# First loads, idle run and late steps of an FNet-plus-mixer kernel: another order of queues, places and turns

## The chip, the cores and the metric

The kernel runs on one core of a Trainium2 chip. The time is device microseconds of one execution, from the program's start to its end; a figure for a kernel is the median of several executions. Engines are called by their names: TensorE (PE, with its weight loads as PEld), VectorE (DVE), ScalarE (ACT), GpSimd (POOL) and SyncE (SP), which here only issues transfers. Transfers that SP and ScalarE issue go to a queue of their own each; those that GpSimd issues go to a third.

## What is computed

The input `x` is one matrix of 2048 tokens by 640 channels. With `xn` the layer norm of `x` over the channels, the output is the sum of three terms:

```python
xn = _layernorm(x)
# A: FNet. Real(DFT_seq(DFT_hid(layernorm-ed x))), as real matrices
a = einsum("bsd,ed->bse", xn, dft_hid_re);  b = einsum("bsd,ed->bse", xn, dft_hid_im)
A = einsum("ts,bse->bte", dft_seq_re, a) - einsum("ts,bse->bte", dft_seq_im, b)
# B: Mixer over the tokens, shared by the channels
h = _layernorm(xn)
u = gelu(einsum("bsd,sf->bdf", h, w1) + b1)          # F = 1728
B = transpose(einsum("bdf,fs->bds", u, w2) + b2)
return x + A + B
```

All is float32. There are four large products: two with the sequence matrices (2048 by 2048 each), one with the hidden matrices (640 by 640), and the two layers of the mixer (2048 by 1728).

## The kernel before

**Arithmetic.** Each float32 operand is cut in two: a high part, which ScalarE makes (`high`, line 151), and a low part, which VectorE makes by subtraction (`low`, line 154). A block product is three TensorE matmuls (`three`, lines 162, 163 and 165): high by high, high by low, low by high. Beyond the first columns, products of 2 by 2 blocks are done with seven instead of eight block products; the sums and differences of blocks that this needs are made on VectorE (`sub`, line 157). An operand block that comes from memory and is cut for one use is a *piece*.

**Steps.** The program is one list of steps. A step is one piece and the matmuls that use it. `turn_of(i)` (line 1215) writes out, for step `i`, in this order: transfers (`loads`), reads of finished banks (`reads`), sums (`sums`), the high cut of the piece for step `i + 2`, `extras`, `timed` actions, one or no waiting *job*, the low cut of that piece, and the matmuls of step `i`. So pieces are cut two steps ahead. Each engine executes its share in exactly this order. Jobs prepare operands for a later stage; they stand in one first-in-first-out list and are taken one for each turn, where the tables `JOBS_AT` and `LONG_AT` allow it. A `None` in the list uses up a turn and does nothing.

**Stages.** The first columns of the sequence product (lines 487 to 577, steps 0 to 9), six further groups of columns and the last halves (`columns`, line 579), the hidden product (`hidden`, stage "hid", written with `row_steps`), the first mixer layer in two passes (`up(0, r)` and `up(1, r)`, r from 0 to 6), and the second in two passes (`down(0, t)`, `down(1, t)`). The sequence product goes out to DRAM as `y`, in part by accumulating stores on GpSimd's queue, and is read again by the hidden stage (line 1033). Half results of the mixer's first layer are kept in DRAM as `up`.

**The start.** The word list `START` (line 49) writes out the first turns by hand. Among its words: `x0` loads row block 0 of `x` and `b0` the first piece of the sequence matrix (`load`, line 494); `M`, `A`, `R` take a row's statistics, their aggregate and the root; `D` and `H` write the row's high parts, `L` its low parts, `N` normalizes it; `T` and `B` cut a piece's high and low part; `P` runs matmuls, with `-0-1` or `-2` naming which of the three. Ahead of `START` stand a few instructions: the second half of row block 0 on ScalarE's queue (line 135), two clears on VectorE, a dummy activation that loads ScalarE's table (line 142), and `WARM` matmuls on a cleared tile, the idle run (line 148).

**Places.** Large tiles live in fixed places: `slab0` to `slab7`, which hold the normalized rows' parts first and the moving operands of the later stages after; `xa` and `xb` for pieces; `ca`, `cb`, `v` and the three parts `x0`, `x1`, `x2` of `xb` for pairs of row blocks. A new tile in a place waits until the old one's last reader is done. The long group of columns (the fourth) needs two more pairs of pieces than its place holds; they stand in a slab under the name `more` (line 598). The hidden matrices wait in a slab as `hids` (line 766) and are cut to operands by `matrices` (line 774). Lines 1165 to 1196 say which slab or place each of these takes, and when.

**Second passes.** `rows_again` (line 784) loads rows of `x` once more (line 790), normalizes them a second time and cuts them for the first mixer layer. In `up(1, r)` the result is added to what pass 0 left in DRAM by an accumulating load (line 1050), and `gelu` follows some turns later (lines 1052 to 1066). For r from 4 to 6 the result goes to DRAM again (line 1070), and `hidden_rows` (line 795) fetches it for the second pass of the last layer.

Of the kernel before, what the change touches and what calls it, by code (L numbers as in the profile page):

```python
# [8 lines left out]
F32 = mybir.dt.float32  # L9
R32 = mybir.dt.float32r  # L10
BF16 = mybir.dt.bfloat16
AF = mybir.ActivationFunctionType
ALU = mybir.AluOpType

P = 128
S = 2048
D = 640
# [8 lines left out]
CH = 512  # L26
NC = S // CH
H2 = D // 2
# [3 lines left out]
WARM = 10  # L32
# [17 lines left out]
    x0 b0 x1 b1 b2 x4 b3 x5 b4 x2 x3 b5 x6 x7 b6 b7  # L50
    M0 A0 R0 T0 D0 O0 V0 H0 B0 M1 A1 T1 B1 N0 R1 T2 L0 O1 V1 H1 B2 P0-0-1 P1-0-1 P0-2 P1-2
# [26 lines left out]
def fnet_plus_mixer(  # L78
# [56 lines left out]
    nc.scalar.dma_start(x_in[0][:, H2:], x_rows[0][:, H2:])  # L135
# [3 lines left out]

    nc.vector.memset(one, 1.0)  # L140
    nc.gpsimd.memset(eps, EPS)
    nc.scalar.activation(one, one, AF.Abs_reciprocal_sqrt)
    nc.gpsimd.tensor_scalar(idea, eps, EPS, eps, op0=ALU.add, op1=ALU.mult)
    idle = keep.tile([P, CH], BF16, name="idle", tag="slab7")
    nc.vector.memset(idle, 0.0)
    psum = [acc.tile([P, CH], F32, name=f"psum{i}") for i in range(8)]
    for i in range(WARM):
        nc.tensor.matmul(psum[7], idle[:, :P], idle, start=True, stop=True)
# [338 lines left out]
    def first_columns():  # L487
# [6 lines left out]
        def load(i):  # L494
            m, k = FIRST[i][:2]
            nc.sync.dma_start(raw[:, FIRST_AT[i], :], dft_seq[m * NC, k])
# [33 lines left out]
        def row(k):  # L530
            if k == 0:
                nc.sync.dma_start(x_in[0][:, :H2], x_rows[0][:, :H2])
            else:
                nc.sync.dma_start(x_in[k], x_rows[k])
# [27 lines left out]
        def whole_row(k):  # L562
# [13 lines left out]
            "L": lambda k: first_rows(k, 1),  # L576
        }

    def columns(g, h, c):
# [13 lines left out]
        def load(name, q):  # L593
            i, m = int(name[1]) - 1, int(name[2]) - 1
            k = 8 * h + q + 4 * i
            if q >= 4:
                if not more_pairs:
                    more_pairs.append(keep.tile([P, 2, 2, 2, CH], F32, name="more", tag="slab1"))
                k = APART + q - 4 + 4 * i
            nc.sync.dma_start(b(name, q), dft_seq[m * NC + c, k])  # L600
# [163 lines left out]
    def load_matrices(qs):  # L764
        if 0 in qs:
            t = keep.tile([P, 3, 2, D], F32, name="hids", tag="slab0")
            raw_hid.update({q: t[:, q] for q in range(3)})
        for q in qs:
            if q > 2:
                raw_hid[q] = place["v"]()  # L770
            for m in range(2):
                nc.sync.dma_start(raw_hid[q][:, m, :], dft_hid[m, q])
# [22 lines left out]
    def hidden_rows(q, at):  # L795
        return from_place(at, lambda v: nc.sync.dma_start(v, part_up[4 + q]), [], "down1", q, f"slab{q}")
# [240 lines left out]
    def up(stage, r, at):  # L1037
# [6 lines left out]
        def end(c):  # L1044
# [19 lines left out]
            late = 5 if tail else 2 if r >= 4 else 1  # L1064
            for i in range(2):
                timed[e + 6 + late + i].append(lambda i=i: gelu(i))
            if r < 4:
                timed[e + 9].append(lambda: jobs.extend(moving_of("down0", r, f"slab{4 + r}", lambda: c)))
            else:
                timed[e + 8 + late].append(lambda: nc.gpsimd.dma_start(part_up[r], c))  # L1070
# [4 lines left out]
        def by_dram(i):  # L1075
            def run(row, half, b):

                at = i in (5, 7)
                t = place["x1"]()[:, (r + (i in (5, 4))) % 2, at * H2 : (at + 1) * H2]
# [82 lines left out]
    for q in range(3):  # L1162
# [3 lines left out]
        [j for q in range(4) for j in matrices(q, f"slab{(q + 1) % 4}")] + factors_again() + [lambda: load_matrices((4,))]  # L1166
# [6 lines left out]
    for q in range(4):  # L1173
        get, changes, rest = rows_again(0, q, "v")
        timed[s_hid - 1].append(lambda js=[get, None, None] + changes + rest: jobs.extend(js))
# [13 lines left out]
    for r in range(NF2):  # L1189
        up(1, r, ("x2", "ca", "cb", "v", "x0")[r % 5])  # L1190
# [3 lines left out]
    gets_hid, _, rests_hid = zip(*(hidden_rows(q, ("x0", "v")[q % 2]) for q in range(3)))  # L1194
    for q in range(2):
        timed[s_down + 7 + 2 * q].append(lambda q=q: jobs.append(gets_hid[q]))
# [98 lines left out]
```

## Time and profile before

| | |
|---|---|
| Median of 3 executions | 867.07 us (866.6 to 867.45) |
| The profiled execution | 867.25 us, with a span of 865.5 us from the first to the last instruction |
| TensorE busy | 860.3 us, 4894 matmuls |
| VectorE busy | 693.4 us |
| ScalarE busy | 525.4 us |
| Transfers | 154.44 MB, mean 178 GB/s |

How to read the rows that follow. A row of the timeline has the start and the length in us, the engine, the line of the kernel, the operation, the tile written and the tile read, shapes, how many instructions are drawn together, and in brackets the idle time before it with what ended that idle time. "SPq", "ACTq" and "POOLq" are the issuing of transfers. A row of the waits names who waited, for whom, and the total, number and longest of these waits. A row of the windows names a stretch, its length, the busy time and number of instructions of PE, PEld, DVE, ACT and POOL, the granted clock, the share of the transfer engines and their GB/s. A row of the transfers by issue ends with the KB of one and the median time from issue to landing.

### The profile page before, as it was taken

The page shows a single profiled execution, that of the slowest core. Times are in us where ns is not written, and L with a number is a line of the kernel's source. Part 1 is how long each engine was busy: PE and PEld are TensorE (multiplying, and loading weights), DVE is VectorE, ACT ScalarE, POOL GpSimd, SP SyncE. Part 2 cuts the span into 40 slices and gives each one's busy share as a digit, 9 for nine tenths or more (in the row PEclk, how much of TensorE's full clock was granted, in tenths as well). Part 3 has the DMA queues.
Part 4 walks back from the last instruction along what each step waited for, and adds up shares of the span by engine and source line. Part 5 has one row for each costly group of instructions (what it writes and reads, how often), then busy time and mean ns, then how long its engine had stood idle before and what let it go on. Part 6 is the DMA issues. An engine that isn't in the chain of part 4 may idle for free.

```text
span 865.5 us, 13906 instructions
## 1 busy us (share of the span) xinstructions
PE 860.3 (99%) x4894; PEld 788.9 (91%) x4894; DVE 693.4 (80%) x1172; ACT 525.4 (61%) x975; POOL 162.6 (19%) x224
## 2 busy tenths in 40 slices
PE   9999999999999999999999999999999999999998
PEld 6888888888888888888999999999999999999998
DVE  7798868758768888677877788888678978987887
ACT  6765576763555555547565556676667866555654
POOL 4222131210020211122110101111312221101211
PEclk9999999999999999999999999999999999999999
DMA  9949596795382746879586766665687789766776
GB/s 345 360 100 270 185 252 228 161 285 160 98 186 29 201 98 140 206 115 190 111 182 155 165 138 196 189 170 162 143 187 169 162 233 241 183 142 125 157 170 149
DMA packets 90293, 154.44 MB, mean 178 GB/s; under 512 B 9008, under 2 KB 37424, under 8 KB 89968
## 3 DMA queue, kind: packets, MB, share of 16 engines
q0 software_dynamic: 25008, 57.52, 36.8%
q1 hardware_dynamic: 64928, 95.80, 33.9%
q8 instruction: 38, 0.62, 0.3%
q14 instruction: 31, 0.25, 0.1%
q10 hardware_dynamic: 288, 0.25, 0.1%
HBM read 99.96 MB, written 58.82 MB: 183 GB/s over the span
## 4 chain that ended last, share of the span: by engine, by line
PE 98%; DMA 1%; ACT 0%; DVE 0%; issue 0%; DVEq 0%; ACTq 0%
PE psum L163 32%; PE psum L162 32%; PE psum L165 31%; PE psum L508 3%; DMA y<-c 1%; DMA x<-in_x 0%; ACT piece L151 0%; DVE st L223 0%; ACT shid L151 0%; ACT c L671 0%; ACT pair L954 0%; DVE pair L946 0%; DVEq L1291 0%; DVE mv L226 0%; ACT near L232 0%
## 5 line engine op out<-in xcount | busy, mean ns | idle before, releaser
L151 ACT ACTIVATE piece<-pieces 128x512 fp32r<-128x512 f32 (+2 forms) x472 | 295.6, 626 | 222.1 <-PE psum L165 139.2
L154 DVE TENSOR_TENSOR piece<-pieces,piece 128x512 fp32r<-128x512 f32 (+4 forms) x496 | 327.2, 660 | 128.2 <-ACT piece L151 124.9
L162 PE MATMUL psum<-piece,n 128*128 128x512 f32 x540 | 210.1, 389 | 0.0
L163 PE MATMUL psum<-piece,n 128*128 128x512 f32 x540 | 210.1, 389 | 0.0
L165 PE MATMUL psum<-piece,n 128*128 128x512 f32 x540 | 210.1, 389 | 0.0
L162 PE MATMUL psum<-sup,piece 128*128 128x320 f32 x392 | 120.8, 309 | 0.0
L162 PE MATMUL psum<-sdown,piece 128*128 128x320 f32 x392 | 120.8, 309 | 0.0
L163 PE MATMUL psum<-sdown,piece 128*128 128x320 f32 x392 | 120.8, 309 | 0.0
L163 PE MATMUL psum<-sup,piece 128*128 128x320 f32 x392 | 120.8, 309 | 0.0
L163 PEld LDWEIGHTS psum<-piece,n 128*128 128x128 f32 x540 | 101.4, 188 | 21.1
L165 PEld LDWEIGHTS psum<-piece,n 128*128 128x128 f32 x540 | 101.3, 188 | 21.1
L162 PEld LDWEIGHTS psum<-piece,n 128*128 128x128 f32 x540 | 101.3, 188 | 20.9
L157 DVE TENSOR_TENSOR pieces<-pieces 128x512 f32<-128x512 f32 (+3 forms) x142 | 111.9, 793 | 3.0
L165 PE MATMUL psum<-sup,piece 128*128 128x320 f32 x368 | 113.7, 309 | 0.0
L165 PE MATMUL psum<-sdown,piece 128*128 128x320 f32 x368 | 113.7, 309 | 0.0
L485 POOL DMA_DIRECT2D y<-c x65 | 56.0, 891 | 255.2 <-DVE c L683 153.9
L162 PE MATMUL psum<-shid,piece 128*128 128x320 f32 x280 | 86.6, 309 | 0.4 <-ACT pair L954 0.4
L165 PE MATMUL psum<-shid,piece 128*128 128x320 f32 x280 | 86.5, 309 | 0.0
L163 PE MATMUL psum<-shid,piece 128*128 128x320 f32 x280 | 86.5, 309 | 0.0
L162 PEld LDWEIGHTS psum<-sup,piece 128*128 128x128 f32 x392 | 73.6, 188 | 0.0
L162 PEld LDWEIGHTS psum<-sdown,piece 128*128 128x128 f32 x392 | 73.6, 188 | 0.0
L163 PEld LDWEIGHTS psum<-sdown,piece 128*128 128x128 f32 x392 | 73.6, 188 | 0.0
(129 smaller groups left out, 1110.5 us busy)
## 6 DMA issues: line engine op xcount, KB each, us to landing
pieces<-in_dft_seq SPq DMA_DIRECT2D x120, 256.0 KB, 5.3
y<-c POOLq DMA_DIRECT2D x105, 256.0 KB, 4.8
pieces<-in_w SPq DMA_DIRECT2D x88, 256.0 KB, 4.0
out<-pair POOLq DMA_DIRECT2D x38, 320.0 KB, 5.9
pieces<-y SPq DMA_DIRECT2D x32, 320.0 KB, 4.5
pieces<-in_w SPq DMA_DIRECT2D x32, 192.0 KB, 2.7
out<-in_x SPq DMA_DIRECT2D x16, 320.0 KB, 8.0
up<-pair POOLq DMA_DIRECT2D x8, 640.0 KB, 3.2
```

The costliest lines, as they stand in the source:

```text
L151: nc.scalar.activation(hi, src, AF.Copy)
L154: nc.vector.tensor_sub(lo, src, hi.bitcast(F32))
L157: nc.vector.tensor_sub(to, a, b)
L162: nc.tensor.matmul(psum, wh, mh, start=first, stop=False, skip_group_check=True)
L163: nc.tensor.matmul(psum, wh, ml, start=False, stop=last and wl is None, skip_group_check=True)
L165: nc.tensor.matmul(psum, wl, mh, start=False, stop=last, skip_group_check=True)
L485: nc.gpsimd.dma_start(y_part[m][c][:, j, :], t, accum_op=ALU.add)
L508: nc.tensor.matmul(banks[m, j], channels(k, j)[rows], w[cols], start=n == 0 and k == begin, stop=n == 2 and k == end, skip_group_check=True,)
```

## The change

The diff touches the start and the order of some late steps. No matmul of the computation is added or taken away.

- **Row block 0.** Both halves are loaded on SP's queue, one after the other. The first piece goes on ScalarE's queue instead of SP's, behind a one-column clear of its place on VectorE, so its issue waits for that clear.
- **Start order.** The table-loading activation becomes a word of its own, `W0`, after `b0`. The second piece is loaded before row block 1, and its cuts `T1 B1` are written ahead of row 1's statistics `M1 A1`.
- **Idle run.** The cleared tile has 128 instead of 512 columns and is cleared first. The run has 14 matmuls instead of 10: ten of 512 columns, which read the tile four times over, and four of 128.
- **Slabs.** The late pairs' pieces (`more`) take slab 0 and the hidden matrices slab 1; the cut matrices' slabs go along.
- **Later turns.** The two gelus of `up(1, r)` are one step later except at the last r; so are the job list's next entries and the store. In `rows_again(0, q)` the load comes one job later, and the second normalization as late as before. The second fetch of `hidden_rows` is two steps later.
- **Places.** `x0`, `x1`, `x2` and `v` trade roles in `up` and `hidden_rows`.

```diff
-WARM = 10
+WARM = 14
...
-    x0 b0 x1 b1 b2 x4 b3 x5 b4 x2 x3 b5 x6 x7 b6 b7
-    M0 A0 R0 T0 D0 O0 V0 H0 B0 M1 A1 T1 B1 N0 R1 T2 L0 O1 V1 H1 B2 P0-0-1 P1-0-1 P0-2 P1-2
+    x0 b0 W0 b1 x1 b2 x4 b3 x5 b4 x2 x3 b5 x6 x7 b6 b7
+    M0 A0 R0 T0 D0 O0 V0 H0 B0 T1 B1 M1 A1 N0 R1 T2 L0 O1 V1 H1 B2 P0-0-1 P1-0-1 P0-2 P1-2
...
-    nc.scalar.dma_start(x_in[0][:, H2:], x_rows[0][:, H2:])
...
+    idle = keep.tile([P, P], BF16, name="idle", tag="slab7")
+    nc.vector.memset(idle, 0.0)
     nc.vector.memset(one, 1.0)
     nc.gpsimd.memset(eps, EPS)
-    nc.scalar.activation(one, one, AF.Abs_reciprocal_sqrt)
...
-    idle = keep.tile([P, CH], BF16, name="idle", tag="slab7")
-    nc.vector.memset(idle, 0.0)
...
     for i in range(WARM):
-        nc.tensor.matmul(psum[7], idle[:, :P], idle, start=True, stop=True)
+        n = 4 if i < WARM - 4 else 1
+        to = psum[7][:, : n * P].rearrange("p (n c) -> p n c", n=n)
+        nc.tensor.matmul(to, idle, idle.unsqueeze(1).to_broadcast([P, n, P]), start=True, stop=True)
...
-            nc.sync.dma_start(raw[:, FIRST_AT[i], :], dft_seq[m * NC, k])
+            to = raw[:, FIRST_AT[i], :]
+            if i == 0:
+                nc.vector.memset(to[:, :1], 0.0)
+            (nc.sync if i else nc.scalar).dma_start(to, dft_seq[m * NC, k])
...
-                nc.sync.dma_start(x_in[0][:, :H2], x_rows[0][:, :H2])
+                for i in range(2):
+                    nc.sync.dma_start(x_in[0][:, i * H2 : (i + 1) * H2], x_rows[0][:, i * H2 : (i + 1) * H2])
...
+            "W": lambda k: nc.scalar.activation(one, one, AF.Abs_reciprocal_sqrt),
...
-                    more_pairs.append(keep.tile([P, 2, 2, 2, CH], F32, name="more", tag="slab1"))
+                    more_pairs.append(keep.tile([P, 2, 2, 2, CH], F32, name="more", tag="slab0"))
...
-            t = keep.tile([P, 3, 2, D], F32, name="hids", tag="slab0")
+            t = keep.tile([P, 3, 2, D], F32, name="hids", tag="slab1")
...
-            late = 5 if tail else 2 if r >= 4 else 1
+            late = 5 if tail else 3 if r >= 4 else 2
...
-                timed[e + 9].append(lambda: jobs.extend(moving_of("down0", r, f"slab{4 + r}", lambda: c)))
+                timed[e + 10].append(lambda: jobs.extend(moving_of("down0", r, f"slab{4 + r}", lambda: c)))
...
-                t = place["x1"]()[:, (r + (i in (5, 4))) % 2, at * H2 : (at + 1) * H2]
+                t = place["x1" if stage else "x2"]()[:, (r + (i in (5, 4))) % 2, at * H2 : (at + 1) * H2]
...
-        [j for q in range(4) for j in matrices(q, f"slab{(q + 1) % 4}")] + factors_again() + [lambda: load_matrices((4,))]
+        [j for q in range(4) for j in matrices(q, f"slab{(0, 2, 3, 1)[q]}")] + factors_again() + [lambda: load_matrices((4,))]
...
-        timed[s_hid - 1].append(lambda js=[get, None, None] + changes + rest: jobs.extend(js))
+        timed[s_hid - 1].append(lambda js=[None, get, None] + changes + rest: jobs.extend(js))
...
-        up(1, r, ("x2", "ca", "cb", "v", "x0")[r % 5])
+        up(1, r, ("x0", "ca", "cb", "v", "x2")[r % 5])
...
-    gets_hid, _, rests_hid = zip(*(hidden_rows(q, ("x0", "v")[q % 2]) for q in range(3)))
+    gets_hid, _, rests_hid = zip(*(hidden_rows(q, ("v", "x0")[q % 2]) for q in range(3)))
...
-        timed[s_down + 7 + 2 * q].append(lambda q=q: jobs.append(gets_hid[q]))
+        timed[s_down + 7 + 4 * q].append(lambda q=q: jobs.append(gets_hid[q]))
```

## The prediction, made before the changed kernel ran

> **What bounds the kernel now.** I read the page's busy rows first, then the waits of TensorE, then the start and the one stall in the middle at full resolution, and last the chain of waits.
>
> ```profile
> span 865.5 us, 13906 instructions
> PE 860.3 (99%) x4894; PEld 788.9 (91%) x4894; DVE 693.4 (80%) x1172; ACT 525.4 (61%) x975; POOL 162.6 (19%) x224
> PE psum L148 <- DVE idle L145: 1.2, 1, 1.2
> PE psum L508 <- ACT piece L151: 0.4, 1, 0.4
> PE psum L162 <- ACT pair L954: 0.4, 1, 0.4
> 860.00:863.00 3.00, 2.32 (x16) 2.05 (x14) 2.37 (x7) 0.00 (x0) 0.00 (x0) 1.00 0.47 163
> 600.00:700.00 100.00, 100.00 (x684) 100.00 (x683) 81.33 (x138) 71.97 (x143) 24.75 (x30) 1.00 0.74 173
> ```
>
> TensorE is busy 860.3 of 865.5 us. It waits three times in all: 1.2 us before the idle run, 0.4 us between the idle run and the first product, 0.4 us once more at 404.9 us. The rest is the tail: the last matmul ends near 862.3 us (2.32 us of work in the stretch from 860), then the last output goes out. The window from 600 to 700 us, where most moved steps lie, has 100.00 of 100.00 us busy with 684 matmuls, 0.146 us each. No edit removes a real product, so the only time that can be won is in these gaps and in the 4.16 us of idle matmuls ahead of the first product. Much more can be lost: any new wait of TensorE counts in full.
>
> The start, in order of time (start, length, engine, what):
>
> ```profile
> 0.75 0.41 ACTq L135 DMA_DIRECT2D x<-in_x  x1
> 0.76 0.39 SPq L532 DMA_DIRECT2D x<-in_x  x1
> 0.91 0.27 DVE L145 MEMSET idle<- 128x256 uint32 x1
> 1.19 1.28 ACT L142 ACT_TABLE_LOAD   x1 [1.19 <-PEq L1284]
> 1.24 4.16 PE L148 MATMUL psum<-idle 128*128 128x512 bf16 x10 [1.24 <-DVE idle L145]
> 3.69 0.89 DVE L223 BATCH_NORM_STATS2 st<-x 128x6 f32<-128x320 f32 x2 [2.50 <-DMA x<-in_x]
> 4.61 0.21 DVE L226 BATCH_NORM_AGGREGATE mv<-st 128x2 f32<-128x12 f32 x1
> 4.91 0.29 ACT L232 ACTIVATE near<-mv,eps 128x1 f32<-128x1 f32 x1 [2.23 <-DVE mv L226]
> 5.12 0.61 ACT L151 ACTIVATE piece<-pieces 128x512 fp32r<-128x512 f32 x1
> 5.80 10.54 PE L508 MATMUL psum<-piece,n 128*128 128x512 f32 x45 [0.40 <-ACT piece L151]
> x<-in_x ACTq DMA_DIRECT2D x1, 160.0 KB, 3.1
> x<-in_x SPq DMA_DIRECT2D x1, 160.0 KB, 2.9
> 9.50:20.00 10.50, 10.50 (x47) 8.70 (x47) 8.64 (x25) 8.38 (x15) 5.94 (x15) 1.00 1.05 393
> ```
>
> The first product at 5.80 us hangs on a chain that begins with row 0: both halves are issued at once on two queues and land 2.9 and 3.1 us later, at about 3.7 and 3.8 us; then come two statistics, the aggregate, the root on ScalarE, and only behind the root in ScalarE's order the cut of the first piece. The idle run ends at 5.40 us, so row 0 sets the start, by 0.40 us.
>
> **The change, part by part.**
>
> *Row 0 in turn, first piece on ScalarE's queue.* The two halves shared the engines, so each took the time of both. One half is 160 KB, 0.41 us at the 393 GB/s of the row above. Alone in front, the first half should land up to 0.4 us earlier, and the first statistic start at about 3.3 us instead of 3.69. The second half is issued one SP issue (0.39 us) later, just when the first statistic (half of 0.89 us) is busy; it may land at 3.7 us and cost nothing. The aggregate, the root and the cut follow 0.4 us earlier at best: first product at 5.40 us. Against it: the first piece (256 KB) now sits in the other queue, issued behind a one-column memset on VectorE, at about 1.2 us, the moment of the second half's issue. If the engines alternate between the two, the second half lands where it did, at 3.8 us, and behind the 4.1 us at which the second statistic began, so nothing is won; if the piece goes ahead, 0.3 us is lost. I take 0.3 us won, because the second half follows the first in a queue that is already flowing while the other must start, and keep -0.3 and +0.4 as ends.
>
> The Trainium skill (DMA: Bandwidth & Descriptors, section Issuing engines are not separate DMA queues) says that transfers started by different engines run on the same 16 DMA engines and interleave; the two halves landing 0.2 us apart agrees. By that rule the piece takes turns with the second half, the gain would be near nothing, and the sum would be that of the first rival below.
>
> *Longer idle run.* The idle tile is cleared first and at a quarter of its size, so the run can begin at about 0.95 to 1.0 us instead of 1.24. Ten long matmuls are 4.16 us; the four short ones are a quarter of 0.42 us each, 0.42 us at most. The run then ends between 5.2 (1.0 plus 4.16, with four short ones hidden in the modelled end of the last long one) and 5.6 us. It could itself hold back the first product by up to 0.2 us against 5.40. With the chain at 5.50 and the run at about 5.5 us, 0.3 us stays.
>
> *Table load behind the piece's issue (W0), second piece ahead of row 1.* ScalarE now issues the piece (0.41 us) before the table load of 1.28 us and its 0.20 us dummy; they end near 3.1 us, and the next use is the root at 4.5 us. The cover is that 1.4 us; without it the root is late one for one. SP issues as many transfers as before: one half in, one piece out. Row 1 goes behind the second piece (256 KB, 0.65 us at 393 GB/s), and so do its statistics on VectorE behind that piece's low cut. This is the second gate of the start:
>
> ```profile
> 6.50 0.88 DVE L223 BATCH_NORM_STATS2 st<-x 128x6 f32<-128x320 f32 x2
> 7.73 0.69 DVE L154 TENSOR_TENSOR piece<-pieces,piece 128x512 fp32r<-128x512 f32 x1
> 8.71 0.90 DVE L154 TENSOR_TENSOR n<-x,n 128x512 fp32r<-128x512 f32 x2 [0.29 <-ACT x L278]
> 9.45 6.69 PEld L508 LDWEIGHTS psum<-piece,n 128*128 128x128 f32 x30 [0.19 <-DVE n L154]
> ```
>
> The low half of row 0 (8.71 us) already arrives with nothing to spare: the weight load at 9.45 us waited 0.19 us for it. It waits for ScalarE's normalization, which hangs on row 0 as well and moves with it; on VectorE it is queued behind the second piece's cut (0.69), row 1's statistics (0.88) and aggregate (0.21). If row 1 starts them at 7.05 to 7.3 us (6.50 plus 0.65, or a little later behind the cut), they end by 8.4 us and the low half still moves ahead by 0.3 us; if row 1 comes 0.5 us later still, the low half is back at 8.9 us and eats the gain and 0.2 us more. I take 0.05 us off. Start in all: 0.25 us won, between 0.3 lost and 0.4 won.
>
> *Row loads one job later.* The stall at 404.9 us:
>
> ```profile
> 397.18 7.56 DMA y<-c
> 404.84 0.44 ACT L954 ACTIVATE pair<-psum 128x320 f32<-128x320 f32 x1 [1.25 <-DMA y<-c]
> 400.96 2.62 SPq L790 DMA_DIRECT2D pair<-in_x  x2
> 403.63 8.60 SPq L1033 DMA_DIRECT2D pieces<-y  x4
> SPq L790 <- DVE shid L154: 7.9, 1, 7.9
> y<-c POOLq DMA_DIRECT2D x105, 256.0 KB, 4.8
> q8 instruction: 38, 0.62, 0.3%
> 400.00:404.90 4.90, 4.90 (x33) 4.59 (x31) 3.85 (x6) 2.51 (x5) 1.73 (x2) 1.00 1.01 181
> ```
>
> The first block of the new stage (line 954) writes where accumulating stores of y were read from, and one of those took 7.56 us where the median is 4.8. Meanwhile SP stood 7.9 us before the row load of line 790, which waits for VectorE to leave its place; the next read of y (line 1033) stood behind it until 403.63. Moved one job, the row load comes after that read in SP's order. The row load itself does not start later, since VectorE, not the order, releases it at 400.96; but the read of y (320 KB) is free to run before it, into the very time of the slow store, with the engines full (share 1.01). So the edit can lengthen what it sits beside. Ends: at the median the store lands at 402.0 us, ScalarE is free at 403.6, and the 0.40 us stall is gone; with 320 KB wholly in front at 181 GB/s the store is 1.8 us later. A second influence: 38 instruction loads (0.62 MB) serve, by their number, some 257 of the 9,788 TensorE instructions each; four more matmuls with their weight loads are 8 instructions, and move each such load ahead by 8/2 x 0.225 us = 0.9 us. One may be what held the store; which way it turns is open. I take no change, nearest to the row as it is, with -0.4 and +1.8 us as ends. Behind a late line 954 on ScalarE stands the cut of the piece two steps on, 0.7 us, with over a step (15 x 0.146 = 2.2 us) to spare. The normalizations that use the loaded rows come as late as before, two jobs behind instead of three; if a load is not there, ScalarE stands up to one step, 2.2 us, against the same reserve.
>
> *Late pieces in slab 0, matrices in slab 1.* SP stood for the old place:
>
> ```profile
> SPq L600 <- PE psum L165: 7.3, 1, 7.3
> 170.00:177.50 7.50, 7.50 (x35) 6.21 (x34) 3.43 (x5) 6.41 (x11) 2.60 (x3) 1.00 0.84 157
> 177.50:195.00 17.50, 17.50 (x78) 14.48 (x78) 10.41 (x21) 11.05 (x22) 2.50 (x4) 1.00 1.03 331
> L1055 ACT ACTIVATE pairs<-pairs,b_sb 128x640 f32<-128x640 f32 x6 | 4.9, 822 | 0.0
> SPq L796 <- DMA up<-pairs: 11.0, 1, 11.0
> ```
>
> Slab 0 is left one step earlier than slab 1, six matmuls of 0.225 us (17.50 over 78), so SP moves on 1.35 us earlier. TensorE did not wait there (17.50 of 17.50), so nothing is won; if the earlier burst pushed another load back by 1.35 us, the two-step lead of the cuts covers it.
>
> *Gelus and stores a step later, places swapped, later read of the hidden rows.* No instruction is added. A gelu of 0.82 us moves by one step of 12 x 0.146 = 1.75 us, and the jobs behind it by one turn; the store behind it on the POOL queue too. The hidden rows that SP waited 11.0 us for are asked for two steps later. Cover: their first use is seven or more steps away; uncovered, each would cost up to a step, 1.75 us. Taken at nothing.
>
> Sum: 867.25 us is the profiled execution's own time (span 865.5). 867.25 - 0.25 + 0 = 867.0. That execution lies 0.18 above the median of 867.07, so against the median: **866.8 us**.
>
> **Rivals.**
> 1. The start gains nothing (chance 0.2): the piece's turns with row 0's second half, or row 1 in front of the low half, give it back. For it: the shared landing times and the 0.19 us wait; against it: VectorE's 0.29 us idle before the low half. 867.07 + 0 to 0.2: 867.15 us.
> 2. Slower: the read of y now runs ahead of the row load into the slow store at 397 us (chance 0.25). It decides as soon as that store lands later than 405 us. For it: the 7.9 us SP wait that held it back; against: the earlier instruction load. Stall 1.2 to 2.2 instead of 0.4, less the start: 867.6 to 868.6, at half of it 868.0 us.
> 3. The stall vanishes, the store landing before 403.6 us (chance 0.15): 866.8 - 0.4 = 866.4 us.
> 4. The products begin slow (chance 0.05). Idle matmuls come every 0.41 us, products of the same width every 0.23 (3.70 over 16, the row below), and the turn comes during the idle run. Were it to come as much later again, 3.3 us into the products, 1.65 us is lost: 868.4 us. The same can strike before.
>
> ```profile
> 1.24:4.50 3.26, 3.26 (x8) 1.18 (x9) 0.81 (x2) 1.44 (x2) 0.00 (x0) 1.00 0.80 256
> 5.80:9.50 3.70, 3.70 (x16) 2.95 (x17) 3.27 (x8) 2.69 (x5) 2.17 (x5) 1.00 1.03 380
> ```
>
> The Trainium skill (TensorE: Matmul & The Clock Gate, section What's actually happening) has the gate decide in windows of some 3.4 us that run free of the kernel; that makes rival 4 a matter of the run's luck, and the shift of 0.24 us in the idle run's start next to irrelevant.
>
> **How the numbers follow.** The forecast has 0.35, the rivals 0.2, 0.25, 0.15 and 0.05. A difference under 0.2%, 1.7 us, is about what a measurement of this kernel can't tell from none. Faster by more would need more than the stalls at 404.9 and 5.4 us together, so 0.03. Slower by more (over 868.8) takes the upper part of rival 2, rival 4 at its worst, or a stall that none of my rows shows: 0.12. Range: from rival 3 with the best start (866.1) down a little for spread, to the top of rival 2: 866.0 to 868.7. The likeliest case alone: 866.5 to 867.2.
>
> **What would show it.** Right: first statistic near 3.3 us, first product at 5.4 to 5.6 us with no gap behind the idle run, the weight load of the low half near 9.2 us, the read of y ahead of the row load near 397 us, a stall of 0 to 1 us near 405, no other TensorE wait. Wrong: a TensorE wait inside the first 35 us, a stall over 2 us at 405, or any wait between 500 and 862 us.

## The result and the profile after

| | before | after |
|---|---|---|
| Median of 22 executions each, same chip | 867.01 us (866.48 to 867.73) | 868.05 us (867.78 to 868.8) |
| Ratio after to before | | 1.0013 (95%: 1.0007 to 1.0019) |
| Profiled execution, its span | 867.25 us, 865.5 us | 868.05 us, 866.3 us |
| The 17th product (counted from 0) begins | 9.79 us | 10.55 us |
| The last matmul begins | 862.01 us | 862.37 us |
| From there to the end of SP's last instruction, 0.05 us before the span's end | 3.42 us | 3.87 us |

The change costs 1.04 us, 0.13%. The time lies in the forecast range, but the forecast had the wrong sign: 0.25 us faster was expected. The difference is below the 0.2% that I had set as the bound for one measurement; with 22 executions of each kernel the interval nevertheless leaves 1 out.

Matmul by matmul the two profiles part at three places and meet at one: 0.76 us are lost before the 17th product, 0.68 us are won back near 405 us, 0.28 us are lost near 693 us, and 0.45 us behind the last matmul. 0.76 - 0.68 + 0.28 + 0.45 = 0.81 us, the difference of the spans (865.47 and 866.28 us).

The timeline of the start, kernel after (start, length, engine, line, operation, tiles, shapes, idle time before):

```profile
0.75 0.86 SPq L536 DMA_DIRECT2D x<-in_x  x2
1.01 4.88 PE L148 MATMUL psum<-idle 128*128 128x512 bf16 x14 [1.01 <-DVE pieces L498]
1.01 0.38 ACTq L499 DMA_DIRECT2D pieces<-in_dft_seq  x1
3.17 0.49 DVE L223 BATCH_NORM_STATS2 st<-x 128x6 f32<-128x320 f32 x1 [2.21 <-DMA x<-in_x]
4.30 0.49 DVE L223 BATCH_NORM_STATS2 st<-x 128x6 f32<-128x320 f32 x1 [0.63 <-DMA x<-in_x]
5.13 0.29 ACT L232 ACTIVATE near<-mv,eps 128x1 f32<-128x1 f32 x1 [2.22 <-DVE mv L226]
5.33 0.61 ACT L151 ACTIVATE piece<-pieces 128x512 fp32r<-128x512 f32 x1
6.02 3.88 PE L511 MATMUL psum<-piece,n 128*128 128x512 f32 x14
6.03 0.82 POOL L248 TENSOR_SCALAR beside<-mv,near 128x1 f32<-128x1 f32 x1
6.12 0.68 DVE L154 TENSOR_TENSOR piece<-pieces,piece 128x512 fp32r<-128x512 f32 x1
6.94 0.80 POOL L249 TENSOR_SCALAR beside<-beside,near 128x1 f32<-128x1 f32 x1
7.00 0.69 DVE L154 TENSOR_TENSOR piece<-pieces,piece 128x512 fp32r<-128x512 f32 x1 [0.21 <-ACT piece L151]
8.51 0.92 ACT L278 ACTIVATE x<-x,norm 128x640 f32<-128x640 f32 x1 [1.54 <-POOL norm L243]
10.21 6.90 PEld L511 LDWEIGHTS psum<-piece,n 128*128 128x128 f32 x31 [0.28 <-DVE n L154]
```

The first half of row 0 gains 0.52 us (3.17 against 3.69). The second half loses: its statistic waits 0.63 us on the transfer. The piece on ScalarE's queue was issued at 1.01 us, the second half only at 1.19 us, behind the issue of the first, so the piece came in between. The root starts 0.22 us later than before, and so does the first product (6.02 against 5.80).

The rest is on GpSimd, which works out the factors of row 0's normalization with one tiny operation after the other. In the same view of the kernel before:

```profile
5.81 0.82 POOL L248 TENSOR_SCALAR beside<-mv,near 128x1 f32<-128x1 f32 x1
5.90 0.68 DVE L154 TENSOR_TENSOR piece<-pieces,piece 128x512 fp32r<-128x512 f32 x1
6.72 0.27 POOL L249 TENSOR_SCALAR beside<-beside,near 128x1 f32<-128x1 f32 x1
7.75 0.92 ACT L278 ACTIVATE x<-x,norm 128x640 f32<-128x640 f32 x1
```

A factor takes 0.27 us, also beside row 1's statistics, and 0.80 to 0.82 us beside a low cut, a subtraction of two tiles on VectorE (0.65 to 0.91 us over all profiles of this study). Before, only line 248 met one. The new order `T1 B1 M1 A1` puts the second cut where line 249 runs, and that one takes 0.80 us too. The normalization starts 0.76 us later (8.51 against 7.75), the low half and its weight load (10.21 against 9.45) with it.

Near 405 us, ScalarE's timeline of the kernel after:

```profile
403.60 0.74 ACT L151 ACTIVATE piece<-pieces 128x640 fp32r<-128x640 f32 x1 [0.84 <-DVE pieces L157]
404.35 0.44 ACT L959 ACTIVATE pair<-psum 128x320 f32<-128x320 f32 x1
```

The first block of the stage starts behind a cut, no longer behind a store, and the stall of before is absent. Near 693 us a new one appears. First the window from 690 to 697 us of the kernel before, then of the kernel after (length, then busy time and count of PE, PEld, DVE, ACT, POOL; clock, share of the transfer engines, GB/s):

```profile
690.00:697.00 7.00, 7.00 (x49) 7.00 (x49) 6.36 (x13) 4.47 (x10) 2.56 (x3) 1.00 1.05 309
```

```profile
690.00:697.00 7.00, 7.00 (x48) 6.75 (x47) 5.90 (x12) 4.49 (x11) 3.17 (x4) 1.00 1.05 258
```

PE's own figure is no help, since its ends are modelled; the weight loads show the wait: 6.75 of 7.00 us. What stands in front, in ScalarE's timeline of the kernel before and then of the kernel after:

```profile
689.47 0.43 ACT L1081 ACTIVATE pairs<-psum 128x320 f32<-128x320 f32 x1
689.78 0.42 ACT L151 ACTIVATE piece<-pieces 128x256 fp32r<-128x256 f32 x1
```

```profile
689.28 0.82 ACT L1060 ACTIVATE pairs<-pairs,b_sb 128x640 f32<-128x640 f32 x1
690.00 0.42 ACT L1086 ACTIVATE pairs<-psum 128x320 f32<-128x320 f32 x1
690.32 0.42 ACT L151 ACTIVATE piece<-pieces 128x256 fp32r<-128x256 f32 x1
```

The gelu of line 1060, one step later, now stands in ScalarE's order ahead of a piece's high cut. The cut is 0.54 us later, 0.09 of it from the losses ahead; its low cut follows, and TensorE waits 0.10 us at 692 and 0.18 us at 695 us.

The end, last compute row of the chain of waits, kernel before and then after:

```profile
862.35 0.32 DVE pair L946
```

```profile
862.72 0.32 DVE pair L951
```

The spans end at 865.47 and 866.28 us: 3.12 and 3.56 us behind the start of that row, with the same transfers in between. The view of instructions leaves semaphore waits out; the trace's full list has them. In the kernel after, SP's 592nd instruction is a drain, one of its closing instructions, behind the last of its waits for transfers. SP stands 0.35 us in front of it, and it takes 0.12 us. In the kernel before, the same drain is the 588th; it follows after 0.04 us and takes 0.01 us. That is 0.42 of the 0.45 us. SP has 592 instructions before and 596 after: the same 350 transfers, but four more semaphore waits. In the kernel before the 592nd is the last wait of the final barrier. It takes 0.44 us, but that last wait does so in kernels with fewer and with more instructions too, so a pause can't be seen there.

### The profile page after: what moved, and what is told of

It reads as the page before. It is cut to its first block, busy times and chain, and to the rows that moved or that the text cites. A ratio compares the mean times of both kernels' runs of the same rounds, so it can differ in the third digit from the quotient of the medians.

```text
span 866.3 us, 13917 instructions
## 1 busy us (share of the span) xinstructions
PE 861.5 (99%) x4898; PEld 790.0 (91%) x4898; DVE 693.2 (80%) x1173; ACT 525.7 (61%) x975; POOL 163.3 (19%) x224
## 4 chain that ended last, share of the span: by engine, by line
PE 99%; DMA 0%; DVE 0%; ACT 0%; issue 0%; SPq 0%; DVEq 0%; ACTq 0%
PE psum L162 32%; PE psum L163 32%; PE psum L165 31%; PE psum L511 3%; DMA x<-in_x 0%; ACT piece L151 0%; DVE st L223 0%; SPq L536 0%; DVE pair L951 0%; DVEq L1296 0%; DVE mv L226 0%; ACT near L232 0%; ACTq L232 0%
```

## The experiments

The theory had three places, start, gelu and end; the main rivals were another cause at each of them and chance. All medians are of 11 or 12 executions, and each ratio is against 23 to 35 executions of the kernel before on the same chip. The kernel before has medians from 866.87 to 867.07 us on these occasions, so medians of different occasions can be compared to about 0.2 us.

**Halves of the change.** `late_only` is the kernel before with the later turns, slabs and places of the change; `start_only` has its first-load, start-order and idle-run lines alone.

```diff
-            late = 5 if tail else 2 if r >= 4 else 1
+            late = 5 if tail else 3 if r >= 4 else 2
...
-        timed[s_hid - 1].append(lambda js=[get, None, None] + changes + rest: jobs.extend(js))
+        timed[s_hid - 1].append(lambda js=[None, get, None] + changes + rest: jobs.extend(js))
```

> The kernel before with the late edits alone (slabs, gelus, row loads, places, the later second fetch); the start is the old one. Theory: the late edits are worth about -0.7 us at 405 us (the 0.40 us wait for line 954 goes, and the matmuls behind it move up) and cost about 0.3 us near 692 to 695 us, where a gelu stands in ScalarE's order ahead of a piece's high cut in the last r; so about 0.4 us faster than before, first product near 5.8 us. Rival: the late edits carry the loss, 0.5 us or more slower than before.

> The changed kernel with all late edits undone: only the start is new. Theory: TensorE's products are about 0.75 us later than before from the low half of row 0 on (about step 17 of the products), whatever the clock of the first products, and nothing gives that back; 0.7 to 1.1 us slower than before. Rival (the loss is in the late edits): within 0.3 us of before.

late_only 867.48 us, ratio 1.0005 (0.9996 to 1.0013); start_only 867.38 us, 1.0011 (1.0002 to 1.002). Both expectations missed: the first was to be 0.4 us faster than before, the second 0.7 to 1.1 us slower. By the medians each half loses about half, 0.50 and 0.40 us, but neither loss is resolved. The interval of start_only leaves 1 out only because one of its twelve executions took 871.92 us; the other eleven have a mean of 867.47 us, against 867.03 us of the kernel before. What each half does is read from the profiles. late_only has the waits near 693 us (0.27 us in all) and 3.85 us behind the last matmul's start; start_only has neither (3.45 us), but the 17th product at 10.57 us. The stall at 405 us is gone in both, also where no late line is changed. So the part of the theory that gave the later row loads 0.4 us wasn't borne out; `before_again` below comes back to it.

**Order of the start.** `rows_first` is the kernel after with row 1's statistics ahead again, nothing else:

```diff
-    M0 A0 R0 T0 D0 O0 V0 H0 B0 T1 B1 M1 A1 N0 R1 T2 L0 O1 V1 H1 B2 P0-0-1 P1-0-1 P0-2 P1-2
+    M0 A0 R0 T0 D0 O0 V0 H0 B0 M1 A1 T1 B1 N0 R1 T2 L0 O1 V1 H1 B2 P0-0-1 P1-0-1 P0-2 P1-2
```

> The changed kernel with row 1's statistics (M1 A1) written ahead of the second piece's cuts (T1 B1) again, all else as changed. Theory: GpSimd's second factor instruction (line 249) took 0.80 instead of 0.27 us because VectorE's low cut of the second piece now runs beside it; with the statistics there again it takes about 0.27 us, row 0's normalization starts about 0.5 us earlier (near 8.0 us), and the kernel gains up to 0.5 us on the changed one. Rival: GpSimd's instruction is long for another reason, or row 1 arrives so late that the second piece's cut is then what is late: no gain, and line 249 still near 0.8 us.

867.51 us (867.39 to 867.9), 0.54 us under the kernel after, whose executions range from 867.78. The timeline of its start:

```profile
5.89 0.82 POOL L248 TENSOR_SCALAR beside<-mv,near 128x1 f32<-128x1 f32 x1
6.81 0.27 POOL L249 TENSOR_SCALAR beside<-beside,near 128x1 f32<-128x1 f32 x1
7.84 0.65 DVE L154 TENSOR_TENSOR piece<-pieces,piece 128x512 fp32r<-128x512 f32 x1
7.85 0.93 ACT L278 ACTIVATE x<-x,norm 128x640 f32<-128x640 f32 x1 [1.00 <-POOL norm L243]
```

With the second cut out of the way, line 249 takes 0.27 us again, the normalization starts at 7.85 us and the 17th product at 9.89 instead of 10.55.

**Queue of the first piece.** `piece_on_sp` is the kernel after with that piece behind both halves of row 0 on SP:

```diff
-            if i == 0:
-                nc.vector.memset(to[:, :1], 0.0)
-            (nc.sync if i else nc.scalar).dma_start(to, dft_seq[m * NC, k])
+            nc.sync.dma_start(to, dft_seq[m * NC, k])
```

> The changed kernel with the first piece on SP's queue behind both halves of row 0 (no clear ahead of it). Theory: the piece's issue at 1.01 us on ScalarE's queue came ahead of the second half's at 1.19 us and held its landing at 4.27 us; behind it the second half lands near 3.6 us, the second statistic follows the first without a gap, the root is at 4.5 us instead of 5.13, and the first product at 5.4 to 5.7 us instead of 6.02; 0.3 to 0.6 us faster than the changed kernel. Rival: the first piece itself, landing later, now sets the first product, near 6.0 us, and nothing is gained.

867.06 us, 0.99 us under the kernel after; against before 1.0004 (0.9995 to 1.0012). Its timeline:

```profile
3.04 0.95 DVE L223 BATCH_NORM_STATS2 st<-x 128x6 f32<-128x320 f32 x2 [2.08 <-DMA x<-in_x]
4.34 0.29 ACT L232 ACTIVATE near<-mv,eps 128x1 f32<-128x1 f32 x1 [2.09 <-DVE mv L226]
4.93 0.64 ACT L151 ACTIVATE piece<-pieces 128x512 fp32r<-128x512 f32 x1 [0.30 <-DMA pieces<-in_dft_seq]
5.63 0.80 POOL L249 TENSOR_SCALAR beside<-beside,near 128x1 f32<-128x1 f32 x1
6.53 0.80 POOL L250 TENSOR_SCALAR norm<-beside,near 128x1 f32<-128x1 f32 x1
7.72 0.93 ACT L278 ACTIVATE x<-x,norm 128x640 f32<-128x640 f32 x1 [1.25 <-POOL norm L243]
```

Both statistics run in one go, the root comes 0.79 us earlier than in the kernel after, and now the piece itself, last in the queue, is waited for (0.30 us). Two factors meet a cut here too (0.80 us each), so the slow factors have not gone. But their chain begins 0.79 us earlier, the normalization starts 0.79 us earlier (7.72 against 8.51 us), and the 17th product is at 9.76 us: the two start losses lie on one chain, and an early row 0 pays for a slow factor. The gain is more than the 0.3 to 0.6 us that had been expected, and not all of it is the start: 0.29 us lie behind the last matmul's start (3.58 instead of 3.87 us), for a reason that the runs on the end show below.

**How much is chance.** `before_again` is the kernel before, unchanged, `after_again` the kernel after.

> The kernel before once more, unchanged, for a second profile of it. Theory: the stall behind 404.9 us in the first profile (0.40 us, 0.68 us with the matmuls around it) is a matter of that execution, since the new start alone, without any late edit, was free of it too; here no TensorE wait near 405 us, a last matmul near 861.3 us plus what the late turn of TensorE's clock costs, and 867.0 us. Rival: the stall belongs to this kernel, stands here again, and the late edits do win 0.4 us or more at this place.

> The changed kernel once more, unchanged. Theory: the same two lots of GpSimd's factor chain beside VectorE's subtractions (two instructions near 0.8 us instead of one), the low half of row 0 near 10.1 us and product 17 near 10.5 us whatever the turn of TensorE's clock, waits near 692 and 695 us, 3.8 to 3.9 us from the last matmul to the end, and 868.0 us. Rival: these belong to the first profile alone and at least one of the three is missing here.

before_again 867.23 us, span 865.3 us; after_again 868.06 us, span 866.3 us. The losses of the kernel after stand again at all three places (the 17th product at 10.60 us, the waits near 693 us, 3.85 us at the end). The kernel before shows no stall at 405 us this time: that one belonged to its first profile, and of all sixteen profiles to that one alone. Against this profile of before the last matmul of the kernel after starts 0.57 us later (862.37 against 861.80): 0.45 us at the start, since TensorE's clock turned late in this profile of before and its 17th product came at 10.10 us, and 0.28 us near 693 us, less a stall of 0.17 us near 723 us that the kernel after doesn't have. With 0.45 us at the end that makes 1.02 us, beside 1.04 us of the medians.

Chance isn't all there is to these stalls. Matmul by matmul, five of the seven profiles whose row loads, slabs and second fetch are those of the kernel before have one: 0.68 us at 405 us (`before`), 0.17 and 1.28 us near 723 us (`before_again`, `idle_only`), 0.42 and 0.29 us near 191 us (`gelu_only`, `best_start`). None of the nine profiles with these edits has one. Each stands behind a late transfer. The cuts that waited in gelu_only and in idle_only, from ScalarE's timelines:

```profile
189.23 0.63 ACT L151 ACTIVATE piece<-more 128x512 fp32r<-128x512 f32 x1 [1.95 <-DMA more<-in_dft_seq]
```

```profile
722.47 0.63 ACT L153 ACTIVATE piece<-pieces 128x512 fp32r<-128x512 f32 x1 [2.68 <-DMA pieces<-in_w]
```

`more` is what the change moves to another slab. The late load of `in_w` is the first one behind the second fetch of the hidden rows in SP's order: in idle_only the fetch was issued at 715.08 us and the load at 715.52 us. In the kernel after, where the fetch is asked for later, one such load goes ahead of it, at 710.41 us. Over the seven profiles the stalls come to 0.41 us each on average. So these edits seem to win what the prediction put at nothing, and the three losses hide it. This is a count over single profiles; no run made these edits one by one, so it is not shown which edit removes which stall.

**The gelu.** `gelu_only` is the kernel before with its later step for r from 4 on; `late_gelu_back` is late_only without it:

```diff
-            late = 5 if tail else 2 if r >= 4 else 1
+            late = 5 if tail else 3 if r >= 4 else 1
```

```diff
-            late = 5 if tail else 3 if r >= 4 else 2
+            late = 5 if tail else 2
```

> The kernel before with one edit: the gelus of r = 4 and 5, and the store behind them, one step later (late = 3). Theory: TensorE waits 0.1 us near 692 and 0.18 us near 695 us as in every kernel with all late edits, so 0.27 us more from product 200 to the last than in kernels without it (810.3 instead of 810.05 us, a stall near 405 us set aside); 0.2 to 0.3 us slower than before at most. Rival: it takes the changed places or jobs as well, and no such wait appears.

> The late edits alone, with the two gelus of r = 4 and 5 at their old step (late = 2). Theory: the gelu of r = 4 stood at 689.3 us in ScalarE's order ahead of a piece's high cut in the last r, made it 0.5 us later, and TensorE waited 0.1 and 0.18 us near 692 and 695 us; with the old step no such wait, products 0.28 us earlier from there on, 0.2 to 0.3 us faster than the late edits alone (867.48). Rival: the places or the later store are behind these waits, and they stay.

ScalarE's timeline of gelu_only, its window, and then the window of late_gelu_back:

```profile
688.90 0.82 ACT L1055 ACTIVATE pairs<-pairs,b_sb 128x640 f32<-128x640 f32 x1
689.93 0.42 ACT L151 ACTIVATE piece<-pieces 128x256 fp32r<-128x256 f32 x1
```

```profile
690.00:697.00 7.00, 7.00 (x48) 6.75 (x48) 6.05 (x11) 4.49 (x11) 3.17 (x4) 1.00 1.04 254
```

```profile
690.00:697.00 7.00, 7.00 (x50) 7.00 (x49) 6.36 (x13) 4.47 (x10) 2.56 (x3) 1.00 1.05 301
```

At this point gelu_only is 0.29 us ahead of the kernel before, so its cut, 0.15 us later by the clock of the view, is 0.44 us late, as in the kernel after (0.45 us). The one line brings the waits (6.75 us) and takes them away (7.00 us), in profiles. The medians don't resolve 0.27 us: gelu_only 867.2 us, ratio 1.0005 (0.9996 to 1.0014); late_gelu_back 867.53 us, no less than late_only's 867.48. In late_gelu_back's profile a factor met a cut by chance and the 17th product came at 10.36 us.

**The idle run and another start.** `idle_only` is the kernel before with the change's idle run; `rows_in_turn` is start_only with the piece on SP, with the table load first, and with row 1's load and statistics ahead again; `best_start` is start_only with the piece on SP and one small load moved to ScalarE's queue. One line of each of the last two:

```diff
-    x0 b0 W0 b1 x1 b2 x4 b3 x5 b4 x2 x3 b5 x6 x7 b6 b7
+    W0 x0 b0 x1 b1 b2 x4 b3 x5 b4 x2 x3 b5 x6 x7 b6 b7
...
-    loads[s_hid + 21].append(lambda: nc.sync.dma_start(b2_sb, b2))
+    loads[s_hid + 21].append(lambda: nc.scalar.dma_start(b2_sb, b2))
```

> The kernel before with the new idle run alone (narrow tile cleared first, ten long and four short matmuls). Theory: the first product waits for row 0 as before, at 5.8 us, and the clock turns 3.5 to 6 us after the run's start at a time that differs from execution to execution; same as before within 0.2 us. Rival: the longer run holds back the first product, or brings the clock's turn forward reliably; 0.2 us or more either way.

> A start put together from both: row 0's halves in turn on SP, the first piece behind them on SP, row 1 ahead of the second piece and its statistics ahead of that piece's cuts as before, the new idle run; none of the late edits. Theory: root near 4.4 us, first product near 5.6 us with the low half of row 0 ready in time, no wait inside the first 35 us beyond the clock, and no loss late: 0.2 to 0.4 us faster than before. Rival: the first piece or row 1, now landing later, holds the first products, and it is the same as before or slower.

> The new start with the first piece on SP behind row 0's halves (second piece and its cuts ahead of row 1, as changed), no late edits, and the second bias on ScalarE's queue, so that SP has no more instructions than before. Theory: first product near 5.6 us and product 17 near 9.75 us at a clock turning at 6 us, 810.05 us from product 200 to the last, 3.45 us from the last matmul to the end: 0.2 to 0.5 us faster than before. Rival: the landing of the first piece or the two long GpSimd instructions take the start's gain back, and it is the same as before.

idle_only 867.0 us, 1.0004 (0.9995 to 1.0013): the idle run changes nothing that the times resolve. In its profile the clock turned 2.65 us after the run's start, earlier than the 3.5 us that had been the least expected, and the 17th product came at 9.78 us. rows_in_turn 867.17 us, 1.0003 (0.9994 to 1.0012), first product at 6.08 us, since the piece landed late this time (its cut began at 5.40 us). best_start 867.35 us, 1.0004 (0.9995 to 1.0013), with the first product at 5.61 us in its profile. Both were expected to be at least 0.2 us faster than before, and neither is. An early row 0 brought nothing measurable by itself; in rows_in_turn's profile the piece behind it was what the first product waited for.

**The end.** `late_sp_plus1` is late_only with one more transfer on SP, `after_sp_minus6` the kernel after with six fewer:

```diff
-    loads[s_hid + 21].append(lambda: nc.sync.dma_start(b2_sb, b2))
+    loads[s_hid + 21].append(lambda: [nc.sync.dma_start(b2_sb[:, i : i + 8], b2[:, i : i + 8]) for i in (0, 8)])
```

```diff
-        loads[s_rows + 10 + 8 * (t // 2) + t % 2].append(lambda t=t: nc.sync.dma_start(out_rows[t], x_rows[t]))
+        loads[s_rows + 10 + 8 * (t // 2) + t % 2].append(lambda t=t: (nc.scalar if t >= NS - 4 else nc.sync).dma_start(out_rows[t], x_rows[t]))
...
-    loads[s_hid + 20].append(lambda: nc.sync.dma_start(b1_sb, b1))
-    loads[s_hid + 21].append(lambda: nc.sync.dma_start(b2_sb, b2))
+    loads[s_hid + 20].append(lambda: nc.scalar.dma_start(b1_sb, b1))
+    loads[s_hid + 21].append(lambda: nc.scalar.dma_start(b2_sb, b2))
```

> The late edits alone with one transfer more on SP (the second bias in two halves of eight columns, near 450 us), so that every later instruction of SP is one place further on. Theory: the 0.34 us by which SP is late at the very end, between its last wait and its closing drain, belongs to a place in SP's stream of instructions (the 592nd in all four kernels with the late edits' count); moved by one it lies inside a wait for the last transfer, as in the kernel with the first piece on SP, and the stretch from the last matmul to the end is 3.5 to 3.6 us instead of 3.84. Rival: the pause belongs to the drain or to what the late edits leave unfinished, and stays at 3.84 us.

> The changed kernel with six transfers moved from SP's to ScalarE's queue, all in mid-run (both biases, four row blocks of x to the output); nothing else differs, and SP's 592nd instruction is then in its last barrier, as in the kernel before. Theory: from the last matmul's start to the end 3.4 to 3.5 us instead of 3.86, and 0.3 to 0.4 us faster than the changed kernel (868.05). Rival: the 0.4 us at the end belong to the late edits whatever SP's count, and stay; or the six issues on ScalarE cost as much on the way.

late_sp_plus1 missed: 867.78 us, and 4.23 us at the end where 3.5 to 3.6 had been expected. The extra transfer also changed the order of SP's closing waits: it waited for the last one first and then passed seven others, done long before, at 0.06 us each, with the pause on top. after_sp_minus6 has 867.55 us (867.33 to 868.23), 0.50 us under the kernel after, with the losses at the start and near 693 us still there. Its header and the last compute row of its chain:

```profile
core 0 of [0], span 865.9 us
862.80 0.33 DVE pair L951
```

The last row starts 0.08 us later than in the kernel after, and the span ends 0.34 us earlier. Its late edits are those of the kernel after, so these edits alone don't make the long end. Over all profiles, by the number of SP's instructions (from the trace's list):

```
SP instructions   from the last matmul's start to the end of the last of them, us
590, 591, 592     3.42 to 3.45   (seven profiles)
593               3.55, 3.56     (gelu_only, rows_in_turn)
595, 596          3.85 to 3.87   (late_gelu_back, late_only, rows_first, after, after_again)
597               3.58 (piece_on_sp), 4.23 (late_sp_plus1)
```

The pause stands in front of the 592nd in all nine profiles that have 593 or more (0.34 to 0.38 us); with 592 or fewer no such pause can be told from the barrier's own waits. With 593 it stands in front of a drain inside the barrier, whose last wait is then 0.15 instead of 0.44 us, so it costs 0.1 us. In piece_on_sp it stands on a closing wait that takes 0.23 to 0.25 us in the others anyway, and costs about 0.1 us; with 595 and 596 it stands behind the closing waits and costs 0.4 us. So the length of the end follows SP's count; why SP pauses there stays open.

**All three undone.** `three_undone` is piece_on_sp with the gelus back (`late = 5 if tail else 2`) and the six transfers of after_sp_minus6 off SP.

> The changed kernel with the three losses undone and the rest kept: the first piece on SP behind row 0's halves, the gelus of r = 4 and 5 at their old step, and the six transfers moved off SP. Theory (these three are all of the loss): first product near 5.6 us, 810.05 us from product 200 to the last with no wait near 692, 695 or 723 us, 3.4 to 3.5 us at the end; 866.5 to 866.8 us, 0.1 to 0.5 us faster than before. Rival: something else in the late edits costs as well; it stays at or above the kernel before.

867.12 us, ratio 0.9998 (0.9986 to 1.0009): the loss is gone, and nothing is won, where 0.1 to 0.5 us had been expected. No kernel of this study is measurably faster than the one before. The medians don't simply add up: the first piece alone gave 0.99 us and the end 0.50, all three together 0.93 (868.05 - 867.12). The profiles say why. The 0.99 us hold 0.29 us at the end, which the 0.50 us count again. And in three_undone's profile the first piece landed late and the first product came at 6.33 us, 0.69 later than in piece_on_sp, so that at the 200th product only 0.26 us had been won over the kernel after, instead of 0.80. With 0.27 us at the gelu and 0.44 us at the end that is the difference of the two spans (866.28 and 865.32 us). How often the piece lands late was not measured.

## Why the prediction failed

The sum had 0.25 us won at the start and nothing for all the rest. Against the second profile of the kernel before, the runs showed 0.45 us lost at the start, 0.28 at the gelus and 0.45 at the end, less 0.17 of a stall. Term by term:

**Row 0 in turn.** I took 0.3 us won, "because the second half follows the first in a queue that is already flowing while the other must start". This step failed, with the sign. The first half did come early (0.52 us; 0.4 had been said). But the piece was issued at 1.01 us, because the clear in front of it was done early, and not at the 1.2 us that I had put; it ran between the halves, and the second one landed near 4.27 us. The low end of my bounds, 0.3 us lost "if the piece goes ahead", was right: 0.22. The Trainium skill (DMA: Bandwidth & Descriptors, section Issuing engines are not separate DMA queues) has transfers of different issuers interleave on the same engines; I quoted that and didn't follow it. The trace agrees: the statistics start at 3.17 and 4.30 us with the piece between, at 3.04 us and without a gap in piece_on_sp.

**Second piece ahead of row 1.** I took 0.05 us off, from the room in VectorE's order alone, and called the normalization something that "hangs on row 0 as well and moves with it". This step failed too. The normalization hangs on GpSimd's factors, and these stretch beside a cut; the prediction has no row of POOL in that window. Measured: 0.54 us more (0.76 at the 17th product less the 0.22 of the first), and 0.54 us between the medians of rows_first and the kernel after.

The Trainium skill (SBUF — State Buffer, section Who interferes with whom) has a VectorE operation with two inputs in SBUF contend with a GpSimd operation that reads SBUF, at a shared read port, and has the order of issue decide which of them waits. The 0.27 us that become 0.80 beside a cut of 0.69 us agree with the first part. The recorded start of line 249 (6.94 us) lies just ahead of the cut's (7.00 us), so the trace doesn't show the second part; it shows the cut at its usual length and the factor stretched to just behind the cut's end (spans on GpSimd are rough).

**Longer idle run.** Right at nothing: idle_only can't be told from before. In the kernel after the run ended at 5.88 us, later than the 5.2 to 5.6 us said, and the first product waited for its cut all the same.

**Row loads.** "No change" against the time of the kernel before was right in the medians, by a wrong picture. The read of `y` did go ahead, as foreseen. Rival 2, a longer stall behind the slowed store, didn't come. The store took 6.3 and 6.7 us in the two profiles of the kernel after, 7.6 and 5.0 us in the two of the kernel before. Rival 3 came in the profile, but one profile in seven without the edit has this stall, so its absence shows little. I had built two rivals, 0.4 of the chance, on one row of one execution, without a sign that it comes each time.

**Slab and second fetch.** The step "nothing is won" for the late pieces, and the nothing for the later fetch, rest on a profile in which TensorE didn't wait there. In four others without these edits it did, 0.17 to 1.28 us, and in none of nine with them. The size of that gain isn't resolved by the medians.

**Gelus.** "Taken at nothing", because "their first use is seven or more steps away". That names who waits for the gelu. This step failed: it leaves out who is queued behind the gelu on ScalarE, a cut whose matmuls come soon after. Measured 0.27 us in the profiles, far under the 1.75 us that I gave as the uncovered price.

**The end.** I had no term for it. Measured 0.45 us, about as much as the slow factor.

**The clock.** Rival 4 was small and common: the turn came within the first products in before_again and after, among others (6.47 and 6.91 us). In the kernel before that cost 0.31 us (the 17th product at 10.10 instead of 9.79 us), not 1.65. In the kernel after it cost nothing more, since the low half was late anyway: after_again, whose clock turned at 5.82 us, has the 17th product no earlier (10.60 us).

## What to carry to other kernels

Follow each operand of the first products back over every engine, the nearly idle ones too: here four tiny operations on GpSimd decided the start, and a piece of work moved on VectorE beside them tripled one of them. For a moved instruction ask who stands behind it in its own engine's order, not only who uses its result. Before a stall of one profile becomes a term or a rival, look whether a second execution has it, and measure the stretch behind the last matmul as well: here four more waits on SyncE went with 0.45 us more.

## What was not expected of the hardware

- In all nine profiles with 593 or more instructions on SP, SP stood 0.34 to 0.38 us in front of the 592nd, be it a drain (seven) or a wait (two). What it does there isn't seen.
- SP passes closing waits for transfers that are long done at 0.06 us each.
- TensorE's clock turned between 3.65 and 6.91 us over sixteen profiles, without relation to the idle run's start at 1.00 to 1.24 us.
- Small stalls come and go with the kernel unchanged: 0.68 us at 405 us in one profile of the kernel before, 0.17 us near 723 us in the other.
